# Dense group 0 scored ahead of group 1's transposes, v's overlap read from the next tile, larger early loads, three tail buffers, a patient VectorE queue

## The chip, the cores and the metric

One core of a Trainium2 chip runs the whole program. Its engines are TensorE (PE in the profile; PEld is its weight load), VectorE (DVE), ScalarE (ACT), GpSimd (POOL) and SyncE (SP, which issues every DMA of this kernel). The metric is the device time of one execution in microseconds (us); smaller is better. Three runs of the kernel before took 814.2, 809.76 and 815.52 us, median 814.2.

## The reference

```python
def _attn_ref(q, k, v):                 # (8, 8, 576, 64) float32: B, H, S, D
    q_d = q.reshape(B, H, Sd, 4, D).mean(axis=3)   # and k_d, v_d; Sd = 144
    out_up = np.repeat(sm_attn(q_d, k_d, v_d), 4, axis=2)
    mask = np.abs(pos[:, None] - pos[None, :]) < 4
    scores = np.where(mask, scale * (q @ k.T), -1e9)
    out_local = softmax(scores) @ v
    return out_up + out_local

x = attn_out.transpose(0, 2, 1, 3).reshape(4608, 512)
h = np.maximum(np.maximum(x @ w1, x @ w2), x @ w3)   # 512 -> 768
out = h @ w_out                                      # 768 -> 512
```

Each token attends to the seven tokens around it and, coarsely, to 144 means of four tokens. The sum of the two goes through a layer with three inner matrices of which the largest product counts. The four weight matrices come as float64.

## The kernel before, in words

**Blocks.** The 4608 tokens are done in nine blocks of 512. Block j below 8 is the first 512 tokens of batch element j; block 8 collects the last 64 tokens of all eight. A block has two units, n = 2j and 2j + 1, of four heads each; a unit has two pairs of heads, `pr` 0 and 1. So block 0 consists of units 0 and 1, block 1 of units 2 and 3.

**The MLP of a block** (`mlp_in`, `mlp_out`) is 288 matmuls of 128x512. Its input x and its weights are kept as two float32r parts (`xhi`, `xlo`; `whi`, `wlo`; `hh` and `wo` for the second layer), and each product is the sum of three: high by high, low by high, high by low. `mlp_in` works through six tiles `ft`; each fills three PSUM banks `pm` with 12 matmuls, three for each of the four chunks `c` of x. Chunk c is one pair of heads (units 2j and 2j + 1 give c = 0, 1 and 2, 3), so no bank of a block is complete before the block's last pair is. ACT and DVE take the maximum of the three banks and split it into `hh` (last step: the subtract `hh<-pm,hh` on DVE, 54 in all).

**The weights** are loaded in 24 pieces and turned from float64 bits into two float32r parts (`weight_split`): two ACT and five DVE instructions each, the last subtract (`wlo<-hqk,whi`) on DVE or POOL. Raw pieces are staged in tiles that are idle at that time (`STAGE`: `hh0`..`hh5`, `wo3`..`wo5`, `pv`).

**Attention in two ways.** Blocks 2 to 8 use windows: DVE multiplies k by q for seven shifts (`prod<-k,pq`, 128x1792), reduces (`pq<-prod`), ACT and POOL multiply v by the weights into `pv`, and the seven products are summed into `x`, by DVE in one reduce (`x<-pv`) or by POOL in three adds. Blocks 0 and 1 (`NDENSE = 2`) use the dense way on TensorE: `band_load` and `band_load_v` fetch q, k and v of a unit, `band_transposes` turns q and k (into a tile tagged `whi2` to `whi5`, whose weights come later), `band_scores` multiplies them with a band mask (kept in the tile `prod`), takes maxima (`mxb`) and exponentials into a `wlo` tile, `band_values` multiplies by v. The band of 128 query rows reaches six rows into the next 128, and these are a second small operand of `band_values`, `vb`: before, four loads of six rows for each unit.

**Pooled attention** (`tail_pooled`, `pooled_scores`, `pooled_values`): for the last 32 of the 144 means, raw q, k and v of the unit are fetched one after the other into one tile `traw`, added up in `th` (DVE or POOL), and give `tq` and `vs`. TensorE transposes `tq`; later steps use `pd`, `pdt`, `pt`, `ptt`.

**What sets the order.** Every operation is recorded with a priority (`at`), and the `Recorder`'s `place` then builds each engine's instruction order with a list of costs; where an operation may run on several engines it also picks the engine. Within `place`, an engine takes the ready operation of best priority; `PATIENCE` lets it wait that many ns for a better one rather than start another. On the chip every engine runs its list in order. All instructions are issued through one helper, so all have line L388 and are told apart by tiles.

## Time and profile before

| | |
|---|---|
| three runs | 814.2, 809.76, 815.52 us |
| profiled execution | 810.74 us, span of the core's work 808.9 us |
| busy in the span | PE 759.1, DVE 608.2, ACT 430.5, POOL 310.1 us |
| mean granted TensorE clock | 0.964 |
| DMA | 81.84 MB, mean 101 GB/s |

The span runs from the first to the last instruction of the program; about 2 us of the execution lie around it. A row of a timeline gives start and length in us, engine, operation, tiles (written <- read), shapes, count, and in brackets the idle time of the engine before it and what ended it. A row of busy time by stretch gives, after the stretch and its length, the busy us and instruction counts of PE, PEld, DVE, ACT and POOL, then the granted TensorE clock, the DMA engines' mean busy share and GB/s. A row of waits gives the waiting engine and its result, what it waited for, the total us, how often, and the longest.

### The profile page before, as it was taken

What the parts mean: (1) busy time and instruction counts of PE and PEld (TensorE: products, weight loads), DVE (VectorE), ACT (ScalarE), POOL (GpSimd) and SP (SyncE); (2) the same over time, 40 slices, a digit from 0 to 9 for tenths busy, and PEclk for the clock granted to TensorE, in tenths of its full rate; (3) what the DMA queues carried; (4) which work ended last, traced back from release to release, by engine and by line L of the source; (5) the groups of instructions that cost most, each with busy time, mean ns of one, the idle gap of its engine ahead of it and who ended that gap; (6) DMA issues with size and microseconds to landing.
All of it is one profiled execution on the core that took longest, in us unless ns stands there. A gap on an engine that the chain in (4) does not pass through costs nothing.

```text
span 808.9 us, 12287 instructions
## 1 busy us (share of the span) xinstructions
PE 759.1 (94%) x4008; PEld 595.4 (74%) x4008; DVE 608.2 (75%) x902; ACT 430.5 (53%) x1508; POOL 310.1 (38%) x544
## 2 busy tenths in 40 slices
PE   2797999989999999999989998999899999999997
PEld 1465777767877778687777786777677888888885
DVE  2589995997999999999999999989998741230220
ACT  2486776742685566488367763672667721121111
POOL 0000010123687468299468783783536500000000
PEclk9655999999999999999999999999999999999999
DMA  6695432424334344253335332433242100001002
GB/s 149 158 289 159 96 105 71 160 78 150 89 116 157 108 123 128 69 175 113 114 92 169 113 124 87 158 99 108 82 138 77 34 27 26 1 14 40 0 1 52
DMA packets 74793, 81.84 MB, mean 101 GB/s; under 512 B 30156, under 2 KB 55050, under 8 KB 74730
## 3 DMA queue, kind: packets, MB, share of 16 engines
q1 hardware_dynamic: 74730, 81.07, 33.4%
q8 instruction: 31, 0.51, 0.3%
q14 instruction: 32, 0.26, 0.1%
HBM read 71.61 MB, written 9.44 MB: 100 GB/s over the span
## 4 chain that ended last, share of the span: by engine, by line
PE 37%; DVE 11%; ACT 6%; POOL 6%; issue 5%; DMA 1%; ACTq 0%; DVEq 0%; POOLq 0%
PE pm L388 34%; POOL pv L388 4%; ACT pv L388 3%; PE pa L388 3%; DVE pq L388 3%; DVE prod L388 3%; DVE x L388 2%; DMA v<-in_v_dram 1%; DVE pm L388 1%; DVE t L388 1%; ACT pq L388 1%; DMA traw<-in_v_dram 1%; POOL hqk L388 1%; ACT pa L388 0%; DVE xlo_0r L388 0%
## 5 line engine op out<-in xcount | busy, mean ns | idle before, releaser
L388 PE MATMUL pm<-xhi_0r,whi_0r 128*128 128x512 f32 x648 | 256.0, 395 | 1.6 <-ACT whi_0r L388 1.6
L388 PE MATMUL pm<-xhi_0r,wlo_0r 128*128 128x512 f32 x648 | 255.4, 394 | 1.2 <-DVE wlo_0r L388 1.2
L388 PE MATMUL pm<-xlo_0r,whi_0r 128*128 128x512 f32 x648 | 256.1, 395 | 0.0
L388 POOL TENSOR_TENSOR pv<-v,s 128x256 f32<-128x256 f32 x249 | 148.6, 696 | 48.9 <-DVE s L388 36.1
L388 PE MATMUL pm<-wo_0r,hh_0r 128*128 128x512 f32 x648 | 158.6, 399 | 1.3 <-ACT wo_0r L388 0.7
L388 ACT ACTIVATE pv<-v,s 128x64 f32<-128x64 f32 x572 | 150.1, 409 | 12.5 <-DVE x L388 5.6
L388 PEld LDWEIGHTS pm<-xhi_0r,whi_0r 128*128 128x128 f32 x648 | 122.2, 189 | 28.6 <-ACT whi_0r L388 2.1
L388 PEld LDWEIGHTS pm<-wo_0r,hh_0r 128*128 128x128 f32 x648 | 122.0, 191 | 28.3 <-ACT hh_0r L388 1.5
L388 PEld LDWEIGHTS pm<-xhi_0r,wlo_0r 128*128 128x128 f32 x648 | 122.0, 188 | 27.1 <-DVE wlo_0r L388 1.5
L388 PEld LDWEIGHTS pm<-xlo_0r,whi_0r 128*128 128x128 f32 x648 | 122.2, 189 | 25.1 <-issue 0.9
L388 DVE TENSOR_TENSOR prod<-k,pq 128x1792 f32<-128x1792 f32 x56 | 112.7, 2012 | 6.3 <-DMA k<-in_k_dram 3.5
L388 DVE TENSOR_REDUCE pq<-prod 128x28 f32<-128x1792 f32 x56 | 113.0, 2018 | 3.1 <-ACT pq L388 2.4
L388 DVE TENSOR_REDUCE x<-pv 128x256 f32<-128x1792 f32 x46 | 92.3, 2013 | 8.5 <-PE pa L388 3.4
L388 DVE TENSOR_TENSOR t<-pm,t 128x512 f32<-128x512 f32 x54 | 37.1, 687 | 77.3 <-PE pm L388 77.1
L388 ACT CAST hh_0r<-pm 128x512 fp32r<-128x512 f32 x54 | 31.8, 589 | 96.5 <-DVE pm L388 96.2
L388 POOL TENSOR_TENSOR th<-traw 128x128 f32<-128x128 f32 x38 | 18.7, 491 | 98.2 <-DMA traw<-in_q_dram 62.2
L388 ACT COPY pq<-q 128x256 f32<-128x256 f32 x56 | 21.8, 389 | 62.3 <-DVE pq L388 35.6
L388 DVE TENSOR_TENSOR pm<-pm,t 128x512 f32<-128x512 f32 x54 | 37.5, 694 | 22.9 <-PE pm L388 22.8
L388 ACT COPY y<-pm 128x512 f32<-128x512 f32 x42 | 24.5, 588 | 56.0 <-PE pm L388 54.5
L388 ACT COPY t<-pm 128x512 f32<-128x512 f32 x54 | 31.8, 588 | 32.5 <-PE pm L388 32.2
L388 DVE TENSOR_TENSOR hh_0r<-pm,hh_0r 128x512 fp32r<-128x512 f32 x54 | 37.0, 685 | 11.9 <-ACT hh_0r L388 11.9
L388 POOL TENSOR_TENSOR hv<-v 128x128 f32<-128x128 f32 x49 | 23.8, 488 | 45.8 <-DVE vd L388 33.7
(156 smaller groups left out, 900.9 us busy)
## 6 DMA issues: line engine op xcount, KB each, us to landing
v<-in_v_dram SPq DMA_DIRECT2D x55, 320.0 KB
k<-in_k_dram SPq DMA_DIRECT2D x55, 320.0 KB
out_dram<-y SPq DMA_DIRECT2D x36, 256.0 KB
q<-in_q_dram SPq DMA_DIRECT2D x56, 128.0 KB
hh<-in_moe_w_dram SPq DMA_DIRECT2D x10, 512.0 KB
pv<-in_moe_w_dram SPq DMA_DIRECT2D x5, 512.0 KB
traw<-in_q_dram SPq DMA_DIRECT2D x16, 128.0 KB
v<-in_v_dram SPq DMA_DIRECT2D x16, 128.0 KB
```

The lines of the kernel that those rows point to most:

```text
L388: getattr(self.engines[o.eng], method)(*map(real, args), **{k: real(x) for k, x in kw.items()})
```

## The change

1. In `dense(0)` the order of steps is: transposes of unit 0, scores of unit 0, transposes of unit 1, values of unit 0, scores of unit 1, values of unit 1, then the pooled parts. Before, both units' transposes stood ahead of all scores.
2. The six overlapping rows of v are read from the first six partitions of the next quarter's v tile; only the last quarter's come from a load of its own, one for each block (`vb2[j]`, 6 rows of all eight heads).
3. q and k of unit 1 come as four loads of four heads each into tiles tagged `wo4` and `wo5`, like the other units'; before, eight loads of two heads each into `xhi` and `xlo` tiles.
4. In units 0 to 3 the raw tail q, k and v go into three tiles (`traw`, and the tiles tagged `pd` and `pt`, which later hold the pooled weights of that unit).
5. `FIRST`, the priorities of units 2 and 3, is 42.5 and 42.6 in place of 30 and 35; the constants' priority is -2; `PATIENCE` of DVE is 250 in place of 0; two allocations swap places.

The diff:

```diff
@@ -37,7 +37,7 @@
 LAG0 = 300.0
 SEG = FAC * P
 NDENSE = 2
-FIRST = (0.0, 5.0, 30.0, 35.0)
+FIRST = (0.0, 5.0, 42.5, 42.6)
 WPRIO = (20.0, 60.0, 105.0, 150.0, 160.0, 170.0, 180.0)
 SETS = (5, 4, 3, 2, 5, 4, 5, 5)
 STAGE = ("hh0", "hh1", "hh2", "hh3", "hh4", "hh5", "wo3", "wo4", "wo5", "hh3", "hh4", "hh5", "pv", "pv", "pv", "pv", "hh5", "pv")
@@ -65,7 +65,7 @@
 ENGINES = ("PE", "DVE", "ACT", "POOL", "SP")
 DONE_NS = {"PE": 230.0, "DVE": 150.0, "ACT": 190.0, "POOL": 200.0}
 SPARE = 1000.0
-PATIENCE = {"PE": 0.0, "DVE": 0.0, "ACT": 0.0, "POOL": 0.0, "SP": 0.0}
+PATIENCE = {"PE": 0.0, "DVE": 250.0, "ACT": 0.0, "POOL": 0.0, "SP": 0.0}
 LANES = 8
 SLOW = 70000.0
 
@@ -446,7 +446,7 @@
     early16 = early.bitcast(BF16)
     bandmask = early16[:, : 2 * (P + 6)].rearrange("p (u x) -> p u x", u=2)
     ident16 = early16[:, 2 * (P + 6) : 2 * (P + 6) + P]
-    vb2 = early[:6, 512 : 512 + FAC * HH * D].rearrange("p (u h d) -> p u h d", u=FAC, h=HH)
+    vb2 = [early[:6, 512 + i * 512 : 1024 + i * 512].rearrange("p (h d) -> p h d", d=D) for i in range(NDENSE)]
     vt2 = [new([P, FAC, HH, D], tag=f"wo{i}", name=f"vband_{i}") for i in range(2)]
     wa = [new([P, DM], tag="hqk", bufs=2, name=f"wa_{i}") for i in range(2)]
     whi, wlo = [None] * NFT, [None] * NFT
@@ -544,7 +544,7 @@
         st = state[n]
         tq = st["tq"] = new([P, 2, 2, D], tag="tq", name=f"tq_{n}")
         for g, src in enumerate((q, k, v)):
-            raw = new([P, FAC * D], tag="traw", name=f"traw_{n}_{g}")
+            raw = new([P, FAC * D], tag=("traw", "pd", "pt")[g if n < 2 * NDENSE else 0], name=f"traw_{n}_{g}")
             sp.dma_start(raw, dram(src, ((j * H + h0) * S + FAC * (SD - T32)) * D, [[S * D, HH], [FAC * D, T32], [1, FAC * D]]))
             h = new([P, 2 * D], tag="th", name=f"th_{n}_{g}")
             halves(n, "t", raw, h)
@@ -716,21 +716,16 @@
     def band_load(n):
         j, h0 = n // 2, HH * (n % 2)
         st = state.setdefault(n, {})
+        if n % 2 == 0:
+            sp.dma_start(vb2[j], dram(v, (j * H * S + SEG - 3) * D, [[D, 6], [S * D, H], [1, D]]))
         st["qk"] = {}
         base = (j * H + h0) * S * D
         for w, src in (("q", q), ("k", k)):
-            if n == 1:
-                for pr in range(2):
-                    t = new([P, FAC, 2, D], tag=f"x{'hi' if w == 'q' else 'lo'}{pr}", name=f"{w}4_{n}_{pr}")
-                    for u in range(FAC):
-                        sp.dma_start(t[:, u], dram(src, base + (2 * pr * S + P * u) * D, [[D, P], [S * D, 2], [1, D]]))
-                    st["qk"][w, pr] = t
-            else:
-                t = new([P, FAC, HH, D], tag="pv", bufs=2, name=f"{w}4_{n}")
-                for u in range(FAC):
-                    sp.dma_start(t[:, u], dram(src, base + P * u * D, [[D, P], [S * D, HH], [1, D]]))
-                for pr in range(2):
-                    st["qk"][w, pr] = t[:, :, 2 * pr : 2 * pr + 2]
+            t = new([P, FAC, HH, D], tag="pv" if n != 1 else f"wo{4 if w == 'q' else 5}", bufs=2 if n != 1 else 1, name=f"{w}4_{n}")
+            for u in range(FAC):
+                sp.dma_start(t[:, u], dram(src, base + P * u * D, [[D, P], [S * D, HH], [1, D]]))
+            for pr in range(2):
+                st["qk"][w, pr] = t[:, :, 2 * pr : 2 * pr + 2]
         kh = st["kh"] = new([3, HH, D], tag="kd" if n % 2 else "qd", name=f"kh_{n}")
         sp.dma_start(kh, dram(k, base + SEG * D, [[D, 3], [S * D, HH], [1, D]]))
 
@@ -739,14 +734,9 @@
         st = state[n]
         base = (j * H + h0) * S * D
         vt = st["vband"] = vt2[n % 2]
-        if n % 2:
-            st["vb"] = [new([6, 2, HH, D], tag="k", bufs=2, name=f"vb_{n}_{u}") for u in range(2)]
-        else:
-            st["vb"] = [vb2[:, 2 * u : 2 * u + 2] for u in range(2)]
         for u in range(FAC):
             lo = 3 if u == 0 else 0
             sp.dma_start(vt[lo:, u], dram(v, base + (P * u - 3 + lo) * D, [[D, P - lo], [S * D, HH], [1, D]]))
-            sp.dma_start(st["vb"][u // 2][:, u % 2], dram(v, base + (P * u + P - 3) * D, [[D, 6], [S * D, HH], [1, D]]))
 
     def band_transposes(n, pr, tag):
         st = state[n]
@@ -814,7 +804,7 @@
         prob = st["prob", pr]
         sm = prob[:, :KB].rearrange("p (i u x) -> p i u x", i=2, u=FAC)
         pb = prob[:6, KB:].rearrange("p (i u x) -> p i u x", i=2, u=FAC)
-        vt, vb = st["vband"], st["vb"]
+        vt = st["vband"]
         psb = bank([6, 2, FAC, 32], "pq", f"pstb_{n}_{pr}")
         pts = []
         for i in range(2):
@@ -834,15 +824,15 @@
                 pe.matmul(px[64 * i : 64 * i + 64, u], vt[:, u, 2 * pr + i], pts[i][:, u], start=u == 0, stop=False, tile_position=(0, 64 * i), skip_group_check=True)
         for u in range(FAC):
             for i in range(2):
-                pe.matmul(px[64 * i : 64 * i + 64, u, P - 6 :], vb[u // 2][:, u % 2, 2 * pr + i], pb[:, i, u, 26:], start=False, stop=u == FAC - 1, tile_position=(0, 64 * i), skip_group_check=True)
+                pe.matmul(px[64 * i : 64 * i + 64, u, P - 6 :], vt[:6, u + 1, 2 * pr + i] if u < FAC - 1 else vb2[j][:, h0 + 2 * pr + i], pb[:, i, u, 26:], start=False, stop=u == FAC - 1, tile_position=(0, 64 * i), skip_group_check=True)
         c = h0 // 2 + pr
         xb = blk["band"][c] = new([P, FAC, P], tag="x", bufs=XBUFS, name=f"xb_{j}_{c}")
         copy(xb, px.rearrange("p u (r f) -> p f (u r)", f=FAC))
 
     def band_pooled_values(n):
         j, h0 = n // 2, HH * (n % 2)
+        vd = state[n]["vd"] = new([P, HH, D], tag="vd", bufs=2, name=f"vd_{n}")
         hv = new([P, HH, 2 * D], tag="hv", name=f"hv_{n}")
-        vd = state[n]["vd"] = new([P, HH, D], tag="vd", bufs=2, name=f"vd_{n}")
         for g in range(HH):
             vv = new([P, FAC * D], tag="v", bufs=2, name=f"v_{n}_{g}")
             sp.dma_start(vv, row_tokens(v, j, h0 + g, 0, FAC * D))
@@ -943,7 +933,7 @@
         scores = {n: [(n, band_scores, pr, tag) for pr in range(2)] for n in ns}
         values = {n: [(n, band_values, pr, tag) for pr in range(2)] for n in ns}
         if j == 0:
-            order = [load[a][0], load[b][0], load[a][1], load[b][1]] + turn[a] + turn[b] + scores[a] + scores[b] + values[a] + values[b] + [(a, pooled, 0), (b, pooled, 0)]
+            order = [load[a][0], load[b][0], load[a][1], load[b][1]] + turn[a] + scores[a] + turn[b] + values[a] + scores[b] + values[b] + [(a, pooled, 0), (b, pooled, 0)]
         else:
             order = load[a] + turn[a] + scores[a] + values[a] + load[b]
             order += [turn[b][0], scores[b][0], (a, pooled, 0), values[b][0], turn[b][1], scores[b][1], values[b][1], (b, pooled, 0)]
@@ -967,7 +957,8 @@
             with at(40.0 + state["pieces"] * 1.0):
                 f(x)
 
-    load_constants()
+    with at(-2.0):
+        load_constants()
     dense(0)
     weights(weight_in, 0, 1, 2)
     turn(0)
```

What it does to the engines' lists, at three places. In these rows a tile's name carries its buffer and a running number that differs between the two programs.

**TensorE, start of the program.** `kd` holds three extra rows of k of unit 1, `xhi0`, `xlo0`, `xhi1`, `xlo1` its q and k, `prod` the band mask, `whi5` the transposed q and k of unit 0's first pair, `pd`, `pdt` and `ptail` pooled weights of unit 0. Before, after the first 18 transposes and the pooled scores of unit 0:

```order
L388 MATMUL pm_1_148<-ident_0_98,kd_0_254 128x3 x2
L388 MATMUL pm_2_158<-ident_0_98,xhi0_0_174 128x128 x4
L388 MATMUL pm_3_167<-ident_0_98,xlo0_0_218 128x128 x4
L388 MATMUL pm_0_144<-ident_0_98,xhi1_0_204 128x128 x4
L388 MATMUL pa_0_206<-ident_0_98,pd_0_294 128x128
L388 MATMUL pa_1_231<-ident_0_98,pdt_0_292 128x128
L388 MATMUL pa_1_231<-ident_0_98,ptail0_0_96 128x128
L388 MATMUL pa_0_206<-ident_0_98,pd_0_294 128x128 x3
L388 MATMUL pm_1_148<-ident_0_98,xlo1_0_236 128x128
L388 LDWEIGHTS prod_0_126
L388 MATMUL pm_2_158<-prod_0_126 128x268
```

With the change, straight after the same 18 transposes:

```order
L388 MATMUL pm_0_148<-ident_0_98,pv_1_131 128x128 x4
L388 LDWEIGHTS prod_0_122
L388 MATMUL pm_1_153<-prod_0_122 128x268
L388 LDWEIGHTS prod_0_122
L388 MATMUL pm_2_163<-prod_0_122 128x268
L388 MATMUL pm_1_153<-whi5_0_112 128x134
L388 MATMUL pm_2_163<-whi5_0_112 128x134
L388 MATMUL pm_1_153<-whi5_0_112 128x134
L388 MATMUL pm_2_163<-whi5_0_112 128x134
```

The scores of unit 0 (the rows that read `prod` and `whi5`) stand directly behind the transposes they need; unit 1's transposes begin at row 45 of the list, behind the scores of both pairs of unit 0. Before, they stood behind 14 transposes of unit 1.

**SyncE, the loads behind v of unit 0.** `traw`, `pd` and `pt` take the raw tails of unit 0, `v` the pooled v, `xhi`, `xlo`, `wo4`, `wo5` and `kd` q and k of unit 1. Before:

```order
L388 DMA traw_0_152<-in_q_dram 128x1x256
L388 DMA v_0_162<-in_v_dram 128x256
L388 DMA v_1_169<-in_v_dram 128x256
L388 DMA xhi0_0_174<-in_q_dram 128x2x64 x4
L388 DMA traw_0_152<-in_k_dram 128x1x256
L388 DMA xhi1_0_204<-in_q_dram 128x2x64
L388 DMA v_0_162<-in_v_dram 128x256
L388 DMA v_1_169<-in_v_dram 128x256
L388 DMA xhi1_0_204<-in_q_dram 128x2x64 x3
L388 DMA traw_0_152<-in_v_dram 128x1x256
L388 DMA xlo0_0_218<-in_k_dram 128x2x64 x4
L388 DMA xlo1_0_236<-in_k_dram 128x2x64 x4
```

With the change:

```order
L388 DMA traw_0_142<-in_q_dram 128x1x256
L388 DMA pd_0_144<-in_k_dram 128x1x256
L388 DMA pt_0_146<-in_v_dram 128x1x256
L388 DMA v_0_151<-in_v_dram 128x256
L388 DMA v_1_157<-in_v_dram 128x256
L388 DMA wo4_0_167<-in_q_dram 128x4x64 x4
L388 DMA wo5_0_194<-in_k_dram 128x4x64 x3
L388 DMA v_0_151<-in_v_dram 128x256
L388 DMA wo5_0_194<-in_k_dram 128x4x64
L388 DMA kd_0_229<-in_k_dram 3x4x64
L388 DMA v_1_157<-in_v_dram 128x256
```

The three tails are issued one behind the other, with no load that waits between them, and q and k of unit 1 in eight loads in place of sixteen. The first load of a weight piece (`hh0`) is row 24 of this list; before it was row 49. Up to it stand 38 DMAs, before 71.

**VectorE, where the last chunks of block 0's x are made.** `x_2` and `x_3` are chunks 2 and 3, `t_` + `od` the sum with the pooled part, `xlo` the low part that the matmuls read, `hqk`, `wo4`, `wo5` and `wlo2` weight pieces, `pd` the raw tail k of unit 2. Before:

```order
L388 TENSOR_TENSOR wlo2_0r_75<-hqk_1_549,whi2_0r_71 128x512
L388 SCALAR_TENSOR_TENSOR hqk_0_470<-wo5_0_509,hqk_0_470 128x512
L388 TENSOR_TENSOR vd_1_398<-hv_0_200 128x256
L388 TENSOR_TENSOR t_0_120<-x_2_764,od_0_373 128x512
L388 TENSOR_TENSOR t_1_628<-x_3_832,od_0_373 128x512
L388 SCALAR_TENSOR_TENSOR hqk_0_470<-wo5_0_509,hqk_0_470 128x512
L388 TENSOR_TENSOR q_0_177<-whi5_0_112 128x256
L388 TENSOR_TENSOR qkT_0_179<-q_0_177 128x128
L388 TENSOR_TENSOR xlo2_0r_90<-t_0_120,xhi2_0r_89 128x512
L388 TENSOR_TENSOR xlo3_0r_92<-t_1_628,xhi3_0r_91 128x512
```

With the change:

```order
L388 TENSOR_TENSOR wlo2_0r_73<-hqk_1_406,whi2_0r_71 128x512
L388 SCALAR_TENSOR_TENSOR hqk_0_401<-wo5_0_194,hqk_0_401 128x512 x2
L388 TENSOR_TENSOR th_0_197<-pd_0_144 128x128
L388 TENSOR_TENSOR vd_1_481<-hv_0_209 128x256
L388 TENSOR_TENSOR t_0_120<-x_2_720,od_0_537 128x512
L388 TENSOR_TENSOR tq_0_206<-th_0_197 128x128
L388 TENSOR_TENSOR wlo2_0r_73<-hqk_0_401,whi2_0r_71 128x512
L388 TENSOR_TENSOR t_1_546<-x_3_792,od_0_537 128x512
L388 TENSOR_TENSOR q_0_180<-whi5_0_112 128x256
L388 TENSOR_TENSOR qkT_0_182<-q_0_180 128x128
L388 TENSOR_TENSOR xlo2_0r_90<-t_0_120,xhi2_0r_89 128x512
```

The sums of chunks 2 and 3 are rows 165 and 166 of VectorE's list before and 155 and 158 with the change; the first add on the tail k of unit 2, which waits for a DMA into `pd`, now stands two rows ahead of them.

Over the whole program the lists differ in the choice of engine too: of the 56 sums of window products VectorE does 52 in place of 46 and GpSimd 4 in place of 10 (three adds each); of the products, GpSimd does 261 in place of 249 and ScalarE 524 in place of 572 quarter pieces. The number of matmuls is the same.

## The prediction

> **What bounds the kernel now.** I read the stretches of the span first, then the chain that ended last, then the waits.
>
> ```profile
> 0.00:88.10 88.10, 62.06 (x410) 43.82 (x411) 58.00 (x169) 48.01 (x171) 1.97 (x7) 0.71 0.67 183
> 40.00:80.00 40.00, 35.69 (x239) 24.64 (x239) 35.42 (x89) 28.86 (x102) 1.77 (x3) 0.59 0.72 222
> 40.00:50.00 10.00, 10.00 (x50) 6.24 (x50) 8.33 (x26) 8.59 (x39) 0.00 (x0) 0.50 0.91 295
> 80.00:130.00 50.00, 49.62 (x363) 35.99 (x361) 46.01 (x110) 38.04 (x128) 5.04 (x6) 0.99 0.33 91
> 200.00:600.00 400.00, 386.91 (x1976) 305.02 (x1975) 380.36 (x444) 252.38 (x948) 262.60 (x465) 0.99 0.39 120
> 600.00:809.00 209.00, 202.29 (x940) 165.16 (x939) 75.29 (x103) 59.69 (x173) 25.09 (x39) 1.00 0.09 28
> ...
> 659.39 61.92 PE pm L388 x273
> 721.31 0.44 PE pa L388 x4
> 721.75 81.65 PE pm L388 x360
> ```
>
> From 80 us on TensorE is busy nearly without a break (49.62 of 50, then 386.91 of 400) at a clock of 0.99, and the last 144 us of the chain are its MLP matmuls, 81.65 / 360 = 0.227 us each. VectorE has 75.29 us of work in the last 209. So the end is set by TensorE, and an earlier start of its steady state is worth its full length at the end, as long as VectorE, 95% busy from 200 to 600 (380.36 of 400), can follow. The place to gain is the start: up to 88.1 us TensorE is idle for 26.0 us and VectorE for 30.1.
>
> When does the steady state begin? With chunk 3 of block 0's x, since no bank of the MLP is complete before it.
>
> ```profile
> 73.29 0.79 PE L388 MATMUL pm<-xhi_0r,whi_0r 128*128 128x512 f32 x1
> ...
> 61.69 0.57 ACT L388 COPY x<-pq 128x512 f32<-128x512 f32 x1
> 71.41 0.69 DVE L388 COPY x<-pq 128x512 f32<-128x512 f32 x1
> ...
> 88.12 1.55 DVE L388 TENSOR_TENSOR t<-x,od 128x512 f32<-128x512 f32 x2
> 91.12 1.29 DVE L388 TENSOR_TENSOR xlo_0r<-t,xhi_0r 128x512 fp32r<-128x512 f32 x2
> ```
>
> The first MLP matmul runs at 73.3 us, chunks 0 and 1 are copied out at 61.7 and 71.4, chunks 2 and 3 get their pooled part at 88.1 and are ready at 92.4. What kept VectorE idle until then:
>
> ```profile
> DVE q L388 <- ACT whi L388: 9.0, 1, 9.0
> DVE th L388 <- DMA traw<-in_q_dram: 4.7, 3, 3.1
> DVE th L388 <- DMA traw<-in_k_dram: 4.4, 3, 2.4
> DVE th L388 <- DMA traw<-in_v_dram: 4.4, 3, 2.9
> DVE rd L388 <- ACT pa L388: 2.4, 1, 2.4
> DVE mxb L388 <- PE pm L388: 2.2, 3, 1.0
> DVE ptail L388 <- PEq L998: 0.8, 1, 0.8
> DVE hqk L388 <- ACT hqk L388: 0.7, 1, 0.7
> ```
>
> Nine waits for a raw tail make 13.5 us: one tile, so each load follows the add on the last. The first scores wait too:
>
> ```profile
> 9.04 3.67 PE L388 MATMUL pm<-ident,pv 128*128 128x128 f32 x16
> ...
> 25.16 0.35 SPq L388 DMA_DIRECT2D kd<-in_k_dram  x1
> 26.80 0.37 PE L388 MATMUL pm<-ident,kd 3*128 3x3 f32 x2 [2.86 <-DMA kd<-in_k_dram]
> ...
> 30.84 0.39 PE L388 MATMUL pm<-prod 128*128 128x268 bf16 x2
> ...
> 0.74 0.40 SPq L388 DMA_DIRECT2D ident<-in_ident_dram  x1
> ...
> 10.92 0.68 SPq L388 DMA_DIRECT2D traw<-in_q_dram  x1
> ...
> 15.51 0.29 DVE L388 TENSOR_TENSOR th<-traw 128x128 f32<-128x128 f32 x1 [3.09 <-DMA traw<-in_q_dram]
> ...
> 21.05 4.07 SPq L388 DMA_DIRECT2D xlo<-in_k_dram  x8
> ...
> 41.02 2.11 SPq L388 DMA_DIRECT2D hh<-in_moe_w_dram  x4
> ...
> 46.28 0.66 ACT L388 ACTIVATE hqk<-hh 128x512 f32<-128x512 f32 x1 [0.86 <-DMA hh<-in_moe_w_dram]
> ```
>
> Unit 0's transposes are done at 12.7 us (9.04 + 3.67), yet its band mask is multiplied at 30.8, behind unit 1's transposes, which wait for `kd`, issued at 25.2.
>
> **The change part by part.** *Loads.* SyncE issues the first weight piece at 41.0 us as its 72nd DMA, so one costs (41.02 - 0.74) / 71 = 0.57 us, waits included (0.74 is its first issue). The change has 38 ahead of it: 0.74 + 38 x 0.57 = 22.3 us. It lands 5.3 us later (46.28 - 41.02), so VectorE has weights to split from 27.6 us on, 18.7 us earlier, and they fill its gaps. The 14 small loads of v less, and eight loads of q and k less (4.07 / 8 = 0.51 each), are inside this count. They give nothing of their own at the end.
>
> *Scores ahead of transposes.* Unit 0's scores need only its own transposes, so they start near 14 us in place of 30.8. I walked the lists from there with the durations above: chunk 0 is then copied out near 35 us and chunk 1 near 41, some 27 and 31 us earlier. This is not the gain, because from then on VectorE has the splits of nine weight pieces and unit 1's maxima to do, in list order, ahead of the sums of chunks 2 and 3.
>
> *VectorE up to chunk 3* is therefore the sum that I use. Up to these sums its list holds 65 us of mean durations before and 64 with the change; the trace has 58.0 busy for the first, since instructions overlap, so I take 57.4. Idle time with the change: 9.5 until the first transposes are copied (9.0, and one more DMA of some 0.5 ahead of q), 0.8 before its first instruction, 3 for tails (unit 0's three are issued together and land in one wait, 4.6 us after the issue as at 15.51 - 10.92; unit 1's k and v come while VectorE is busy), 2.4 for `rd`, 2.2 for `mxb` as now, 2 for unit 1's exponentials, 0.7 for a weight piece as now. Sum 20.6, so the sums of chunk 3 come at 78.0 in place of 88.1: **10.1 us earlier**. Bounds: with all 13.5 us of tail waits gone and unit 1's exponentials hidden, 18 us; with the tail waits kept, or moved to another load, 0.
>
> *A wait that is added:* the tail k of unit 2 now goes into `pd`, behind the last transposes that read unit 1's pooled weights and behind v of unit 3, which waits for unit 1's values. Its add stands two rows ahead of the sum of chunk 2 on VectorE. By my walk v's tile is free near 68 us, the load is issued at 70 and lands 4.6 later, at about the time (74 us) when VectorE comes there. I take 0; every us that it is late delays chunks 2 and 3 and all of VectorE's list behind them, up to 4.6 if it is issued only then.
>
> ```profile
> 73.20:92.40 19.20, 9.83 (x26) 5.80 (x26) 0.69 (x1) 0.60 (x1) 0.79 0.61 166
> ```
>
> *TensorE* does as many matmuls as before. When chunk 3 is ready it has done 26 MLP matmuls (this row, of the `pm` tile's instructions alone), and in the changed list 15 stand ahead of the first that needs it, with three more attention matmuls: 11 x 0.227 = 2.5 us less done. The list has scores of unit 2 between, which TensorE does while chunk 3 is summed; I count the difference at 0, with a loss of 2.5 as the other end. After that both lists have the rest of block 0's first layer and of group 1 to do, and from 80 to 130 TensorE alone limits.
>
> *v's overlap from the next tile:* the same 16 small matmuls for a pair, from another tile, whose load the eight matmuls ahead of them need anyway: 0. *Priorities of units 2 and 3:* they let weight pieces go ahead of group 1; its last pair still shares `whi5` with the last weight tile.
>
> ```profile
> 166.49 0.50 PE L388 MATMUL pm<-xhi_0r,whi_0r 128*128 128x512 f32 x1 [1.64 <-ACT whi_0r L388]
> 168.19 0.50 PE L388 MATMUL pm<-xhi_0r,wlo_0r 128*128 128x512 f32 x1 [1.20 <-DVE wlo_0r L388]
> ...
> 187.08 3.07 PE L388 MATMUL pm<-wo_0r,hh_0r 128*128 128x512 f32 x12 [0.67 <-ACT wo_0r L388]
> ```
>
> TensorE waits 3.5 us there for late weights. If all of it goes, -3.5; if the weights keep their old time, the whole gain is waited away at this place. I take 0. *Constants' priority and swapped allocations:* 0, since the first loads are the same.
>
> *Who sums the window products:*
>
> ```profile
> L388 DVE TENSOR_REDUCE x<-pv 128x256 f32<-128x1792 f32 x46 | 92.3, 2013 | 8.5 <-PE pa L388 3.4 <-POOL pv L388 2.7 <-ACT pv L388 0.8
> ...
> L388 POOL TENSOR_TENSOR pv<-pv 128x768 f32<-128x768 f32 x10 | 18.5, 1846 | 0.2 <-ACT pv L388 0.2
> ...
> L388 POOL TENSOR_TENSOR pv<-pv 128x512 f32<-128x512 f32 x10 | 12.5, 1254 | 0.8
> ```
>
> Six more reduces are 6 x 2.013 = 12.1 us for VectorE; GpSimd loses 6 x (1.85 + 1.25) = 18.6 us and the third adds. What hides them: up to the end of block 5 (the 36th subtract of `hh`) the changed list has 42 reduces and 46 products, before 41 and 51, so VectorE has no more to do there; the last four stand behind the 42nd subtract, in the stretch where it is busy 75.29 of 209 us. I take 0; without that cover it is 12.1.
>
> *Patience of VectorE* changes only which instruction stands first. It puts the MLP's maxima ahead of 2 us products that would delay them, at the price of gaps: at most 250 ns by its own estimate for each of 162 MLP steps (three for each of 54), 40.5 us in all, 22.5 of them in the five blocks of 200 to 600 us. The other end is that it removes TensorE's idle time there, 400 - 386.91 = 13.1 us. I take 0, as VectorE's 19.6 us of idle time in that stretch cover most of the one and TensorE's waits are few.
>
> **Sum.** 810.74 - 10 = 800.7 for an execution like the profiled one (808.9 in the span, 1.8 around it). That one lies 3.5 us below the median of the runs shown, 814.2, and their spread is 5.8; the four together average 812.6, and I forecast 812.6 - 10 = 802.6, said as **802 us**. One per cent, 8 us, is about what a measurement can tell from no change here.
>
> **The rivals.** *The gain is waited away (0.24).* Group 1's two units share `whi5`, the last weight tile waits for them, and their loads wait for group 0's tiles; then TensorE idles near 160 us for what it gained. For it: the 3.5 us above, just there. Against it: the weights are loaded 19 us earlier. Some 3 us would stay: 809.6.
>
> *VectorE becomes the bound (0.10).* Place: 200 to 600 us, where a reduce or a gap of patience stands ahead of the subtract that frees a bank. Price: 22.5 us of gaps and 12.1 of reduces, 34.6. It decides once more than the 19.6 us of idle time there is used: 15 over, less 10 gained, gives 817.6; if the idle time can't be used, 812.6 - 10 + 34.6 = 837. Middle 826. Against it: the counts at the 36th subtract.
>
> *Patience pays (0.12).* TensorE's 13.1 us go: 789.5.
>
> *The clock is released (0.06).* In 40 to 50 us TensorE is busy 10.00 of 10 at a clock of 0.50, and 35.69 of 40 at 0.59. If fewer gaps let it run at full clock, those 35.69 us shrink by 0.41 to 21; VectorE still sets chunk 3, but stops waiting for matmuls, 5 to 6 us: 796.5. (The Trainium skill, "TensorE: Matmul & The Clock Gate", section "What's actually happening", has this rule: activity of about 3.4 us releases the throttle. By that rule the stretch of 40 to 50 us should have run at full clock; the row has 0.50, so I give the rule little here.)
>
> **How the numbers follow.** The forecast, 797 to 807, has 0.48; with a tenth of it above 806.1 and the two faster rivals, faster by over 1% has 0.61. The rest of the forecast and the first rival, within 1%, 0.30. Slower by over 1%, above 822.3, 0.09, most of the second rival. The range, 790 to 813, leaves out that rival and the outer ends.
>
> **What would show it.** Right: scores of unit 0 near 14 us, first weight piece issued near 22, tail waits of VectorE near 3 us up to chunk 3, its sums near 78, TensorE's last stretch of MLP matmuls unchanged in length and 10 us earlier. Wrong: a wait of `th` for the load into `pd` ahead of the sums of chunks 2 and 3; waits of over 5 us for `whi` or `wlo` between 140 and 180; more than 25 us of idle TensorE time over the five middle blocks; or unit 1's scores late because SyncE stood at a load.

## The result, and the profile after

The changed kernel takes 800.55 us (median of 4 runs, 800.16 to 800.93) where the kernel before took 813.11 beside it: a ratio of 0.985, 95% interval 0.981 to 0.989, so 1.5% faster. The forecast was 802 us, 10 us less. The profiled execution took 800.16 us, 798.4 of them in the span (810.74 and 808.9 before), so the gain is 12.6 us between the medians and 10.6 between the profiled executions.

The stretches of the changed kernel, with the columns of before (length, then busy time and instructions of TensorE, its weight loads, VectorE, ScalarE and GpSimd, then the granted clock, the DMA share and GB/s):

```profile
0.00:78.00 78.00, 53.02 (x400) 39.24 (x400) 55.73 (x162) 49.29 (x173) 2.48 (x9) 0.76 0.77 211
40.00:80.00 40.00, 30.42 (x232) 21.46 (x228) 36.86 (x92) 28.29 (x97) 0.48 (x1) 0.67 0.73 218
...
80.00:130.00 50.00, 50.00 (x380) 37.40 (x379) 43.27 (x105) 37.40 (x123) 2.69 (x5) 0.99 0.34 101
200.00:600.00 400.00, 389.14 (x1996) 305.09 (x1995) 382.93 (x441) 239.01 (x897) 241.92 (x450) 1.00 0.38 115
600.00:798.40 198.40, 190.75 (x859) 156.30 (x857) 82.94 (x99) 53.63 (x144) 25.70 (x40) 0.99 0.11 34
```

The shape is as before: TensorE has no gap from 80 to 130 us, is busy 389.14 of 400 us in the middle, and the chain of work ends with the same stretch of 360 MLP matmuls in 81.67 us (81.65 before), 10.7 us earlier (711.02 in place of 721.75):

```profile
663.84 46.75 PE pm L388 x206
711.02 81.67 PE pm L388 x360
```

The start has moved. From the timeline of the changed kernel (start, duration, engine, output and inputs, and in brackets a wait):

```profile
9.85 0.70 SPq L388 DMA_DIRECT2D traw<-in_q_dram  x1
10.59 0.55 SPq L388 DMA_DIRECT2D pd<-in_k_dram  x1
11.19 0.52 SPq L388 DMA_DIRECT2D pt<-in_v_dram  x1
...
12.96 0.39 PE L388 MATMUL pm<-prod 128*128 128x268 bf16 x2
...
24.17 1.03 SPq L388 DMA_DIRECT2D hh<-in_moe_w_dram  x2
...
35.86 0.59 ACT L388 COPY x<-pq 128x512 f32<-128x512 f32 x1
...
43.20 0.57 ACT L388 COPY x<-pq 128x512 f32<-128x512 f32 x1
...
66.09 0.80 PE L388 MATMUL pm<-xhi_0r,whi_0r 128*128 128x512 f32 x1
...
73.05 0.55 SPq L388 DMA_DIRECT2D pd<-in_k_dram  x1
...
77.35 0.28 DVE L388 TENSOR_TENSOR th<-pd 128x128 f32<-128x128 f32 x1
...
77.88 0.69 DVE L388 TENSOR_TENSOR t<-x,od 128x512 f32<-128x512 f32 x1
...
79.29 0.68 DVE L388 TENSOR_TENSOR t<-x,od 128x512 f32<-128x512 f32 x1
```

Three tails are issued within 1.9 us, unit 0's band mask is multiplied at 13.0 us (30.8 before), the first weight piece is issued at 24.2 (41.0), chunks 0 and 1 are copied at 35.9 and 43.2 (61.7 and 71.4), the first MLP matmul runs at 66.1 (73.3), and the sum of chunk 3 is made at 79.3 (88.7, the second of the pair that begins at 88.12). What VectorE waited for in the first 78 us of the changed kernel (us in all, times, longest):

```profile
DVE q L388 <- ACT whi L388: 9.7, 1, 9.7
DVE mxb L388 <- PE pm L388: 3.5, 4, 1.6
DVE hv L388 <- DMA v<-in_v_dram: 2.0, 1, 2.0
DVE th L388 <- DMA traw<-in_q_dram: 1.5, 1, 1.5
DVE rd L388 <- ACT pa L388: 1.0, 1, 1.0
DVE ptail L388 <- PEq L989: 0.8, 1, 0.8
DVE th L388 <- DMA pd<-in_k_dram: 0.8, 1, 0.8
```

Waits of `th` for a raw tail are 1.5 + 0.8 = 2.3 us in place of 13.5.

### The profile page after: what moved, and what is told of

Its sections match the earlier page's. It is cut to its first block, busy times and chain, and to the rows that moved or that the text cites. A ratio compares the mean times of both kernels' runs of the same rounds, so it can differ in the third digit from the quotient of the medians.

```text
span 798.4 us, 12177 instructions
## 1 busy us (share of the span) xinstructions
PE 754.2 (94%) x4008; PEld 594.0 (74%) x4008; DVE 628.8 (79%) x910; ACT 417.0 (52%) x1448; POOL 292.7 (37%) x538
## 4 chain that ended last, share of the span: by engine, by line
PE 64%; DVE 17%; issue 4%; ACT 4%; POOL 3%; DMA 3%; ACTq 0%; DVEq 0%; POOLq 0%; SPq 0%
PE pm L388 54%; PE pa L388 9%; DVE prod L388 4%; DVE pq L388 3%; POOL pv L388 2%; DVE hqk L388 2%; ACT pv L388 2%; DVE x L388 2%; DVE xlo_0r L388 1%; DMA traw<-in_v_dram 1%; DVE t L388 1%; PE pq L388 1%; DMA pd<-in_k_dram 1%; DVE nm L388 1%; DVE hh_0r L388 1%
## 5 line engine op out<-in xcount | busy, mean ns | idle before, releaser
L388 POOL TENSOR_TENSOR pv<-v,s 128x256 f32<-128x256 f32 x261 | 154.5, 697 | 73.2 <-DVE s L388 57.4
L388 ACT ACTIVATE pv<-v,s 128x64 f32<-128x64 f32 x524 | 137.8, 412 | 10.7 <-DMA v<-in_v_dram 3.7
L388 PEld LDWEIGHTS pm<-xlo_0r,whi_0r 128*128 128x128 f32 x648 | 122.2, 189 | 25.1 <-issue 0.4
L388 PEld LDWEIGHTS pm<-wo_0r,hh_0r 128*128 128x128 f32 x648 | 119.6, 188 | 27.0 <-issue 1.1
L388 DVE TENSOR_REDUCE x<-pv 128x256 f32<-128x1792 f32 x52 | 104.1, 2012 | 5.8 <-ACT pv L388 4.6
L388 POOL TENSOR_TENSOR th<-traw 128x128 f32<-128x128 f32 x36 | 17.1, 476 | 102.6 <-DVE vs L388 45.8
L388 DVE TENSOR_TENSOR pm<-pm,t 128x512 f32<-128x512 f32 x54 | 37.5, 694 | 20.7 <-PE pm L388 20.6
L388 POOL TENSOR_TENSOR hqk<-k 128x128 f32<-128x128 f32 x48 | 22.2, 463 | 53.4 <-DMA k<-in_k_dram 53.2
```

The lines of the kernel that those rows point to most:

```text
L388: getattr(self.engines[o.eng], method)(*map(real, args), **{k: real(x) for k, x in kw.items()})
```

## The experiments

In each profiled run I read two numbers from the trace: when VectorE starts the sum of chunk 3, and how long it is from there to the end of TensorE's last matmul (792.7 us in the changed kernel, 803.4 before). The table has them for all runs. "Held" are variants of the changed kernel in which every engine's list stays as it is but for the one edit; in the others the planner makes new lists. Each ratio is to runs of the kernel before that were made beside that kernel; their medians lie between 811.4 and 813.1 us.

| kernel | time, us | ratio to before (95%) | chunk 3's sum | from there to the end |
|---|---|---|---|---|
| before | 813.11 | 1 | 88.7 | 714.7 |
| the change | 800.55 | 0.981 to 0.989 | 79.3 | 713.4 |
| held: first load late | 804.42 | 0.990 to 0.994 | 83.6 | 712.5 |
| held: 18 bit operations less | 797.92 | 0.980 to 0.988 | 77.7 | 712.6 |
| held: 9 bit operations more | 804.37 | 0.989 to 0.994 | 84.5 | 711.8 |
| held: TensorE's gaps filled | 801.03 | 0.982 to 0.989 | 81.2 | 713.2 |
| change, old order | 814.74 | 1.002 to 1.006 | 86.5 | 718.6 |
| change, tails in one place | 808.47 | 0.994 to 0.997 | 78.8 | 722.1 |
| change, patience 0 | 807.77 | 0.994 to 0.997 | 76.4 | 722.7 |
| change, patience 200 | 810.57 | 0.997 to 1.001 | 78.0 | 724.4 |
| change, patience 300 | 800.18 | 0.981 to 0.987 | 78.7 | 714.6 |
| change, bit operations left out | 806.1 | 0.992 to 0.997 | 77.2 | 722.2 |
| before, new order alone | 807.53 | 0.994 to 0.998 | 82.5 | 717.2 |
| before, patience 250 alone | 816.81 | 1.004 to 1.008 | 87.1 | 721.7 |

**The first load late.** Four small loads that wait for each other stand ahead of SyncE's first load:

```diff
+            for _ in range(4):
+                self.nc.sync.dma_start(pad[:, :8], src[:, :8])
             for o in out:
```

> The changed kernel with four tiny loads, each waiting for the one before, ahead of SyncE's first load; every engine's list is otherwise the same. They delay the first loads by about 4 x 2 = 8 us. Theory A (the gain is made before block 0's chunk 3 and carried to the end one for one): the whole kernel ends 7 to 9 us later, about 808.5 us, and the 288th MLP matmul moves by the same time. Rival B (some other engine or the later stages set the end and the start has slack): the delay is absorbed, below 804 us.

The first weight piece was issued at 29.00 us in place of 24.17, 4.8 us late and not the 8 expected, so the time lies between the two ranges. The sum of chunk 3 came 4.3 us late and the median rose by 3.9: as theory A has it, most of a delay at the start arrives at the end.

**The bit operations left out.** The two operations of `weight_split` that put the parts of a weight together are gone for all weights, for the planner too:

```diff
-        dve.scalar_tensor_tensor(out=bits, in0=high, scalar=0xC0000000, in1=bits, op0=ALU.bitwise_and, op1=ALU.bitwise_or)
-        dve.scalar_tensor_tensor(out=bits, in0=low, scalar=29, in1=bits, op0=ALU.logical_shift_right, op1=ALU.bitwise_or)
```

> The changed kernel without the two scalar_tensor_tensor steps in the split of each weight piece (the weights' values are then wrong): 2 x 0.68 us of VectorE work less for each of 24 pieces, some 10 us less ahead of the sum of chunk 3. Theory A, in which VectorE's work and idle time set chunk 3: its sum comes 8 to 10 us earlier (near 70 us), and the end 6 to 9 us earlier, 791 to 795 us. Rival C (TensorE at half clock, or the chain scores - exponentials - values, sets chunk 3): chunk 3 moves by less than 3 us and the end stays within 798 to 801 us.

A miss: with less to do for VectorE the kernel became slower than the change, 806.1 us. Chunk 3's sum did come earlier, at 77.2, but the rest took 722.2 us. The planner had made other lists, so this run tells nothing of VectorE by itself; the next two hold the lists.

**18 bit operations less, lists held.**

```diff
                 for method, args, kw in o.forms[o.eng]:
+                    if method == "scalar_tensor_tensor" and kw["op1"] == ALU.bitwise_or:
+                        seen += 1
+                        if seen <= 18:
+                            continue
```

> The change with its lists held word for word, but the two bit operations of VectorE (0.69 us each, 0.60 at their cadence) left out for the first nine weight pieces, all 18 of which stand ahead of chunk 3's sum; the values of these weights are left wrong by that. Theory A (VectorE's serial list up to chunk 3's sum sets the start, and the start carries to the end): 18 x 0.60 = 10.8 us less, of which some is given back to waits; the sum of chunk 3, 79.3 us with the change, comes at 69 to 73, block 0's last MLP matmul at 172 to 176 in place of 181.5, the median at 791 to 795. Theory B (another chain is late right behind VectorE: the tail k of unit 2, whose load is issued at 73.05 and landed at 77.3 just as VectorE came there, or unit 1's values): the sum at 76 to 79, VectorE waiting for th <- pd, the median at 798 to 801.

It is theory B's run, with a median 0.1 us below B's range (the four runs spread from 795.5 to 803.1). The sum came 1.6 us earlier, not 6 to 10, and the timeline shows what VectorE stood at:

```profile
72.68 0.69 DVE L393 TENSOR_TENSOR wlo_0r<-hqk,whi_0r 128x512 fp32r<-128x512 f32 x1
75.79 0.29 DVE L393 TENSOR_TENSOR th<-pd 128x128 f32<-128x128 f32 x1 [2.43 <-DMA pd<-in_k_dram]
76.00 0.42 DVE L393 TENSOR_TENSOR vd<-hv 128x256 f32<-128x256 f32 x1
76.34 0.68 DVE L393 TENSOR_TENSOR t<-x,od 128x512 f32<-128x512 f32 x1
```

It waited 2.43 us for the tail k of unit 2. In the changed kernel the same load is issued at 73.05 and lands at 77.28, and VectorE takes it up at 77.35 without a wait in the record: the two chains end together.

**9 bit operations more, lists held.** The second bit operation of the first nine pieces is issued twice:

```diff
+                    if method == "scalar_tensor_tensor" and kw["op0"] == ALU.logical_shift_right:
+                        seen += 1
+                        if seen <= 9:
+                            getattr(self.engines[o.eng], method)(*map(real, args), **{k: real(x) for k, x in kw.items()})
```

> The change with its lists held, but the second bit operation of the first nine weight pieces done twice, so VectorE has 9 x 0.60 = 5.4 us more ahead of chunk 3's sum. Theory A: the sum at 84 to 85 in place of 79.3, block 0's last MLP matmul 4 to 5.5 us later than 181.5, the median at 804 to 806.5. Theory B (VectorE has room there, another chain sets chunk 3): the sum at 79.5 to 81, the median at 800 to 802.5.

Theory A's numbers, all three: the sum at 84.5, 5.2 us later; the last MLP matmul of block 0 started at 186.8 in place of 181.5; the median 3.8 us higher. So more work on VectorE ahead of chunk 3 delays the kernel at once, and less gains only 1.6 us before the next chain is late.

**Patience 0, 200 and 300, with the change.**

```diff
-PATIENCE = {"PE": 0.0, "DVE": 250.0, "ACT": 0.0, "POOL": 0.0, "SP": 0.0}
+PATIENCE = {"PE": 0.0, "DVE": 0.0, "ACT": 0.0, "POOL": 0.0, "SP": 0.0}
```

> The changed kernel with VectorE's patience back at 0. Theory A: patience is worth little, 799 to 804 us, since the start has the same parts; 47 of the 56 window sums are VectorE's again. Rival D (patience makes the gain, by shorter waits of TensorE in the middle blocks): 808 to 813 us, with TensorE's idle time over blocks 1 to 6 back at 14 us.

> The change with VectorE's patience 200 in place of 250 ns: the lists differ in the middle, the start is nearly the same. Theory P (patience as such is worth the 7 us that the change without it lost): most of it is kept, 799 to 802. Theory M (the 7 us are how the planner deals the middle, and each new deal costs or gives some us): the end of block 0 within 2 us of 181.5, but from there to the end 613 to 619 us in place of 611, the median at 803 to 809.

> The change with VectorE's patience 300 in place of 250 ns. Theory M (each value deals other lists, and 250 is one good deal, not an optimum of a smooth curve: 0 gave 807.8, 200 gave 810.6): 803 to 811, with TensorE's idle time plus its loss to half clock 3 to 9 us above the 59.7 us of the change. Theory P (patience pays from about 250 on): 798 to 802.

807.8 us at 0, 810.6 at 200, 800.6 at 250, 800.2 at 300. At 0 rival D's time was missed by 0.2 us. At 200 theory M's direction holds, and 614.3 us from the end of block 0 to the end lie in its range; but the end of block 0 was 6.5 us late, not 2, and the median is 1.6 us above its range. At 300 theory P holds. Nothing is lost at the start: with 0 and 200 chunk 3's sum is 1 to 3 us earlier than in the change. What is lost comes later. At 0 and 200 TensorE had started only 2 MLP matmuls when chunk 3's sum began, with the change 11, at 300 9, and the middle is thinner too (the rows are patience 0, 200 and 300):

```profile
200.00:600.00 400.00, 383.89 (x1940) 300.01 (x1939) 376.58 (x436) 252.08 (x944) 256.43 (x457) 0.98 0.39 118
200.00:600.00 400.00, 384.71 (x1956) 301.62 (x1955) 381.30 (x430) 236.70 (x876) 249.30 (x452) 0.99 0.38 116
200.00:600.00 400.00, 389.08 (x1984) 305.70 (x1984) 376.74 (x433) 235.57 (x876) 258.80 (x462) 0.99 0.39 116
```

At patience 0 there are 1940 matmul records between 200 and 600 us, where the change has 1996. TensorE is idle there for 16.1 us at 0 and 15.3 at 200, but for 10.9 in the change and at 300. From the end of block 0 to the end patience 0 takes 616.7 us, the change 611.1. Of the 5.6 us between these two profiled executions, 2.7 are idle time of TensorE, and 2.8 are half clock, counted as half of TensorE's busy time at half clock.

**Patience 250 alone, on the kernel before.** The same line, the other way round.

> The kernel before with only VectorE's patience at 250 ns. Theory P (patience as such gives some 7 us): 803 to 806. Theory M (only a new deal): 807 to 816, anywhere around the kernel before, 811.4 to 813.1.

816.81 us, 0.4 to 0.8% slower than before: theory P falls for the kernel before; it lies 0.8 us above M's range. Between 200 and 600 us TensorE is idle for 15.0 us, 13.1 before. Patience does not pay by itself; 250 and 300 do with the new order and loads.

**The old order, with the rest of the change.**

```diff
-            order = [...] + turn[a] + scores[a] + turn[b] + values[a] + scores[b] + values[b] + [...]
+            order = [...] + turn[a] + turn[b] + scores[a] + scores[b] + values[a] + values[b] + [...]
```

> The changed kernel with the old order of steps in dense group 0: transposes of both units ahead of all scores; loads, tails, patience and priorities as in the change. Theory A: unit 0's scores wait for unit 1's q and k again (kd lands near 22 us), chunk 0 comes near 45 us, but VectorE has its tails and weights early; about half the gain is lost, 803 to 808 us. Rival (the earlier loads and tails alone make the gain): within 2 us of the changed kernel, 799 to 802.5 us.

The whole gain was gone, 814.74 us, more than either theory had. Unit 0's band mask came at 25.1 us, and chunk 0 was copied at 59.9, not near 45. Over half of the loss is the start (the sum at 86.5, 7.2 us later), the other part lies behind it (718.6 us in place of 713.4).

**The new order alone, on the kernel before.** The same line in the other direction.

> The kernel before with only the new order of block 0's dense steps (unit 0's scores ahead of unit 1's transposes); loads, tail places, patience and priorities as before. Theory A1 (the order alone carries the gain, since the change without it came out at 814.7): 797 to 803, unit 0's scores near 14 us, the sum of chunk 3 near 80. Theory A2 (order and early loads are needed together: with the first weight piece behind 71 DMAs, at 41 us, VectorE starts the splits late and chunk 3 stays near 86 to 88): 807 to 812. Theory M (how the planner deals the middle weighs as much as the start): the start as in one of these, but from the end of block 0 to the last matmul anything from 610 to 619 us, as in the kernels so far.

807.53 us, the time of theory A2: the order alone gives 0.2 to 0.6%. It brings the sum to 82.5, between the two theories. The first weight piece is still issued only at 42.10 us, and `th` still waits 3.0 + 4.0 + 3.8 us for raw tails. So the order alone gives some 0.4%, the rest without the order nothing (814.74 us), and both together 1.5%; each of these kernels has lists of its own.

**The tails back in one place, with the rest of the change.**

```diff
-tag=("traw", "pd", "pt")[g if n < 2 * NDENSE else 0]
+tag="traw"
```

> The change with the raw tails back in one place (`traw`) for all units, everything else kept. Theory A (the three places are the term that pays: 13.5 us of VectorE's waits for raw tails became 2.3): the tail waits return to 9 to 13 us up to chunk 3's sum, the sum comes at 84 to 89 in place of 79.3, the median at 805 to 810. Theory B (VectorE has weight splits to do while a tail is loaded, now that weights come at 24 us, and the order of scores and transposes carries the gain): tail waits of 3 to 6 us, the sum at 77 to 82, the median at 798 to 804. A figure within 3 us of either can also be a new deal of the lists.

Each theory got half. As B said, the tail waits came back only to 5.1 us (this kernel's waits of VectorE up to 80 us), and chunk 3's sum came at 78.8:

```profile
DVE th L388 <- DMA traw<-in_q_dram: 2.8, 2, 2.2
DVE th L388 <- DMA traw<-in_v_dram: 1.8, 1, 1.8
...
DVE th L388 <- DMA traw<-in_k_dram: 0.5, 1, 0.5
```

Yet the time is A's, 808.47. TensorE's list was another: its first MLP matmul started at 74.9 in place of 66.1, and only one had started when the sum of chunk 3 began, where the change has 11. That is 10 x 0.227 = 2.3 us. Block 0's last MLP matmul started 8.9 us later. Of the other 6.6 us the trace explains 4.7 between the sum and this matmul: 2.1 us more idle time of TensorE, 1.8 of it a wait for `wo` from ScalarE at the end of block 0, and 2.6 us more half clock (it lasts until 82, and comes again at 184.6 for 3.4 us). The rest stays open.

**TensorE's gaps filled, lists held.** Transposes of the identity are issued on TensorE ahead of instructions that wait; the numbers are how many:

```diff
+            fill = {0: (2, 26), 31: (31, 14), 161: (161, 11), 162: (162, 13), 261: (261, 11)}
...
+                            for _ in range(times):
+                                self.nc.tensor.transpose(place, eye[:, :rows], eye)
```

> The change with its lists held, and 75 transposes of the identity added on TensorE where it idled: 26 ahead of its first instruction, 14, 11, 13 and 11 in the gaps at 16.2, 44.6, 47.8 and 71.7 us; they write places that the next real instruction overwrites. Theory D (the clock costs: TensorE lost 18 us to half clock up to the end of block 0, and the gaps bring the half clock): the stretches at half clock, 41.0 us up to 81 us, fall below 25, chunk 3's sum comes at 73 to 77, the median at 793 to 798. Theory A/B (VectorE's list, the tail k and unit 1's pooled values set chunk 3, all three near 77 us, and TensorE's clock hides behind them): the half-clock time may fall, but the sum stays at 77.5 to 79.5 and the median at 798.5 to 801.5. Theory C (the added transposes delay real ones): over 802.

The stretches at half clock up to 90 us were 27.3 us in place of 41.0, and the median stayed: 801.03. One profiled run each does not show that the added transposes did this: the two held kernels with the late load and with 18 operations less have 30.7 us without any, the one with 9 more 54.6. The first 80 us of this kernel, beside 0.67 in the row of the change from 40 to 80 above:

```profile
0.00:40.00 40.00, 31.92 (x243) 26.46 (x245) 21.97 (x77) 22.83 (x83) 2.03 (x8) 0.83 0.78 194
40.00:80.00 40.00, 28.27 (x236) 21.38 (x237) 33.87 (x86) 26.26 (x91) 0.45 (x1) 0.83 0.74 218
```

The time is A/B's, but the sum came at 81.2, 1.9 us late, as theory C has it. The timeline shows why. First the changed kernel, where the band mask of unit 1's second pair follows a gap of 3.40 us; then this one:

```profile
51.16 0.38 PE L388 MATMUL pm<-prod 128*128 128x268 bf16 x1 [3.40 <-ACT wlo L388]
...
51.61 3.04 PE L399 MATMUL pm<-ident 128*128 128x128 f32 x13 [3.55 <-ACT wlo L401]
54.44 0.43 PE L401 MATMUL pm<-prod 128*128 128x268 bf16 x1
```

The 13 transposes meant for this gap did not run in it. They waited for ScalarE as the band mask does in the changed kernel, and then took 3.04 us ahead of it. So these scores came 3.3 us late, and VectorE's `mxb` waited 2.4 us for them. So this run does not decide on theory D: what a free clock gives and what the late scores cost are mixed in it.

The runs of all kernels give only a rough figure. The granted clock differs from run to run of the same kernel, and (1 - clock) x span is the full-clock time that a run lost. The eight runs of the change with the old order lost 9.8 to 33.4 us and took 812.0 to 816.4 us; the one that lost least took 814.6 and the one that lost most 816.3. Over the 75 runs of the 13 other kernels of the table, each taken against the mean of its kernel, a lost microsecond goes with 0.11 us more time (standard error 0.05); without these eight runs it is 0.30 (0.06). If TensorE set the time throughout, it would be 1.

## Why the prediction was right

**The start carries to the end: right, and now shown.** In the five kernels with the same lists chunk 3's sum lies between 77.7 and 84.5 us, and from there to the end it is 711.8 to 713.4 us: the end follows the sum, up to 1.6 us.

**VectorE up to chunk 3: right.** The pair of sums begins at 77.9 where I had 78.0 (88.1 before); chunk 3's own came at 79.3, 9.4 us earlier than before where I had 10.1. VectorE was busy 55.7 us of the first 78 (57.4 in the sum) and idle 22.3 (20.6 in the sum), so that the hit to a tenth is two errors of 1.7 us that cancel. Of the idle terms the tails are 2.3 (3), `rd` 1.0 (2.4), `mxb` 3.5 (2.2); 2.0 for v's tile was not in it, and the 2 for unit 1's exponentials show no wait of that size. Two slips in the working changed nothing: the upper bound comes to 15 us by its own terms (10.1 + 3 + 2), not 18, and the middle of 817.6 and 837 is 827.

**Loads and scores: right in size.** The first weight piece was issued at 24.2 (22.3), since SyncE's DMAs took (24.17 - 0.74) / 38 = 0.62 us each and not 0.57. Scores at 13.0 (14), chunk 0 at 35.9 (35), chunk 1 at 43.2 (41).

**The tail of unit 2 at nothing: right, with its cover used up.** No wait here, 2.4 us as soon as VectorE had 18 operations less ahead of it.

**Late weights: size off.** I took 0 and had 3.5 us as the best case. The waits of TensorE for `whi`, `wlo` and `wo` between 140 and 190 us are gone; this is all that TensorE waited for there:

```profile
PE pa L388 <- POOL kd L388: 0.6, 1, 0.6
```

Against it stands the term of TensorE's matmuls: 11 MLP matmuls started ahead of chunk 3's sum, 20 before, 9 x 0.227 = 2.0 us, near the 2.5 that I had as the other end. From the sum to block 0's last MLP matmul the change takes 102.3 us, before 104.9. Two zeros that partly balance gave the right sum, and that they do is luck.

**The reduces: right.** VectorE does 52, and the last four start between 656 and 668 us, behind the 42nd subtract. Its busy time in the last 198.4 us is 82.94, before 64.85: work moved into the stretch where it has room. From block 0's last MLP matmul to the end it takes 611.1 us, before 609.8.

**Patience at 0: wrong.** The step that failed is the one that priced patience by itself, from gaps on VectorE and idle time of TensorE between 200 and 600 us. The place was right in part, the price was not: taken out of the change it costs 7 us, and TensorE's idle time there is 16.1 us in place of 10.9; given to the kernel before it costs 4, and 200 is no better than 0. The sum was right all the same, because the whole change ends in lists whose time behind chunk 3 is as long as before (713.4 and 714.7), which I had assumed without a reason. With every variant that made the planner deal anew this time was 714.6 to 724.4 us: a zero there has an uncertainty of 10 us, as much as the whole gain. The range reached up by 11, enough for this alone but not beside a start that gains less: the change with the old order took 814.7 us.

**The rivals.** *Waited away at the late weights*: no, the waits went. *VectorE the bound*: no; it is busy 382.93 of 400 in the middle (380.36 before) and TensorE follows. *Patience pays*: not as named, since TensorE's idle time between 200 and 600 us went only from 13.1 to 10.9 us. *The clock is released*: it hardly was (0.67 in place of 0.59 from 40 to 80 us). What a free clock would give stays open: 41.0 us at half clock are 20.5 us lost, and by 0.11 to 0.30 us for each this is 2 to 6 us, an estimate.

What stays open: why the lists of patience 0 and 200 and of the single tail place put TensorE's MLP matmuls later; the planner's decisions were not followed one by one. The start is shown with held lists; what each part of the change gives is not, since every run without a part has new lists. The parts do not add either: taking out the order, the tails or the patience costs 14, 8 and 7 us, together more than twice the gain.

## What to carry to other kernels

Where a planner makes the lists, split the time at the point where the steady state begins: what an edit does ahead of it can be worked out from waits and durations, what it does behind it is a new deal, whose spread is measured with a few neighbours (here three other values of one number gave 800 to 811 us). To test a cause, hold the lists and add or leave out work at one place; a variant that is planned anew tests the planner. Look in the trace whether the added work ran where it was meant to: 13 of 75 transposes did not, and that blurred the answer. And when a stall is removed, look which chains end at the same time: here 11 us less work on VectorE brought the sum 1.6 us earlier.

## What the runs showed of the hardware

TensorE stays at half clock in stretches in which the profile has it busy with hardly a gap. The changed kernel between 20 and 30 us, and the one with a single tail place in two later stretches:

```profile
20.00:30.00 10.00, 10.00 (x56) 7.03 (x57) 6.67 (x23) 8.22 (x44) 0.78 (x2) 0.50 0.92 246
```

```profile
40.00:80.00 40.00, 35.73 (x240) 25.59 (x238) 35.42 (x91) 26.91 (x93) 2.44 (x4) 0.50 0.69 211
50.00:60.00 10.00, 9.58 (x45) 6.75 (x45) 8.82 (x26) 8.79 (x42) 0.32 (x1) 0.50 0.81 249
```

In the changed kernel half clock is recorded from 19.5 for 13.7 us, from 46.8 for 20.5 and from 74.1 for 6.8; each of these begins in a gap of 2.7 to 3.7 us in TensorE's work. In the kernel with one tail place it is recorded from 37.8 for 44.4 us. (The Trainium skill, "TensorE: Matmul & The Clock Gate", section "What's actually happening", has one busy window of some 3.4 us release the clock; the lengths here are multiples of 3.4 us, but a single busy window was not enough, and the rows decide.) The work in these stretches is small matmuls and transposes. Transposes alone can bring the full clock: up to 12.9 us the changed kernel's TensorE does nothing else, and when full clock is first recorded, at 12.7, the time from one to the next drops from 0.21 to 0.11 us; in the kernel with added transposes, which starts 26 of them at 2.56, this comes at 8.2. Why the later stretches stay at half clock is open.

What half clock costs depends on what sets the time. Ahead of chunk 3's sum the changed kernel's TensorE is idle for 25.0 of 79.3 us, and over whole runs a lost microsecond goes with 0.11 to 0.30 us. In the middle, where TensorE is nearly always busy, it is dearer: 2.8 of the 5.6 us that patience 0 lost behind block 0 in its profiled execution are half clock.
